# A new order for the first 512 tokens of a sketched attention with a Swish MLP behind it, and keys turned into a layout with contiguous rows

## The chip, the cores and the metric

The kernel runs on one NeuronCore of a Trainium2 chip. Five engines work side by side, each through its own queue in program order: TensorE (PE in the profile, with its weight loads as PEld), VectorE (DVE), ScalarE (ACT), GpSimd (POOL) and SyncE (SP, which here only issues DMAs). The metric is device time in microseconds of one execution.

## What is computed

Attention with a polynomial sketch: each query and key of 32 numbers is multiplied by two 8x32 matrices, and the 64 products of the two results are its feature vector. Keys and values are summed once per batch and head, and every query reads that sum. The result, 4352 tokens of 128 numbers, goes through an MLP of width 2048 with the gate `h * sigmoid(beta * h)`.

```python
def phi(x):
    a = np.einsum('rd,bhsd->bhsr', S1, x)
    b = np.einsum('rd,bhsd->bhsr', S2, x)
    return np.einsum('bhsi,bhsj->bhsij', a, b).reshape(*x.shape[:-1], r * r)
q_p, k_p = (phi(q), phi(k))
kv = np.einsum('bhsf,bhsd->bhfd', k_p, v)
z = np.sum(k_p, axis=2)
num = np.einsum('bhsf,bhfd->bhsd', q_p, kv)
den = np.einsum('bhsf,bhf->bhs', q_p, z)[..., None] + 1e-06
x = (num / den).transpose(0, 2, 1, 3).reshape(B * S, H * D)
h = x @ w_in
out = (h * (1.0 / (1.0 + np.exp(-beta * h)))) @ w_out
```

There are 4 batches, 4 heads and 1088 positions per head, so 4352 tokens.

## The kernel before

The order of all work is written out by hand in one string of short names, `SEQ`, at the top. Each name issues the instructions of one step on its engines; each engine takes its instructions in that order, and semaphores make it wait for what it reads.

**The attention, per batch b.** `lk`, `lq`, `lv` load keys, queries and values (SP). `tk` turns the keys with DVE transposes (`turn_k`, L456), `kp` multiplies them with the sketches on PE (`kps`, L475), `ka` turns the result back on DVE (`kab`, L492). `ov`/`op` form the 64 products per key on DVE or POOL (`outer`, L513; batch 0 in nine pieces, the others in four), and `v` sums them with the values on PE (L537). Queries: `tq` on DVE (L462), `qp` on PE (L597), `qa` on DVE (L609), denominators `dp` and `di`, a scaling `as`, products `yv`/`yp`, a turn `t` (L640), and `n` on PE (`num`, L653), from which `x` copies tokens into `xT` in fp16 (L665). For batches 2 and 3 the sum z is a DVE reduction `z` (L524) with `zm` on PE and `wz` on DVE; batches 0 and 1 take it from a Gram matrix (`gr` L715, `gc`, `gd`, `wm`, `wc`).

**The first 512 tokens** take a shorter way of their own, named with A: `aA` and `bA` spread the queries on PE (L685), `cA` copies on ACT, `mA` multiplies on DVE, `dA` is the denominator on PE (`den`, L776), `iA` its inverse on DVE, `nA` the numerator on PE (`num0`, L817), `xA` the product of the two on DVE, straight into `xT` (L828).

**The MLP** runs over nine chunks of tokens, eight of 512 and one of 256. A chunk has eight waves: `W` makes two first products of 128x512 on PE into PSUM (`first`, L432; two buffers of that kind), `G` takes the Silu on ACT (L448; 14 buffers for its results), `V` multiplies by the second matrix (`second`, L399). `E` turns the finished chunk on DVE (L413) and stores it. The weights are scaled by beta first: `up`/`uv` (L341, POOL or DVE, after `be` and `bc` spread beta), `wa`/`wp` (L350, L357).

**Warmers.** `h` issues two matmuls on constants into a part of the PSUM tile `kvz0` that nobody reads (`keep_warm`, L191). The same tile holds batch 0's key-value sum.

Two details matter for the change. In `kps` the moving operand is read with an inner step of 288 elements (`kT2` is [token, sketch position] and four tokens far apart are taken together), and in the first pieces of batch 0 ACT copies half of the key sketch into `kvz0` (`acopy0`, L500), from where DVE's `outer` reads it.

In the order before, `SEQ` has batch 1's keys (`tk1`, `kp1`, `ka1`, `gr1`) and batch 0's other queries mixed into the way to the first `W`, and a `V` follows after five `W`s.

Of the kernel before, what the change touches and what calls it, by code (L numbers as in the profile page):

```python
# [9 lines left out]
F32 = mybir.dt.float32  # L10
# [6 lines left out]
P = 128  # L17

SEQ = """
    lk0 lqA lk1 lv0 h sp h h h h sk s1 bsp s0 h sw h tk0a h h h tk0b li0 tqA kp0b li1 kp0a ka0b lq0  # L20
    aA ka0a ca0b li2 op07 h rb ca0a be0 ov06 lo3 cA0 op05 ov08 h lo0 bA bc0 tk1 op04 lo2 gr0 bc1 h
    op02 lk2 h gc0 h be1 ov01 lo1 up0 ov03 h lq1 sr bc2 ov00 v06 up2 v08 lv1 ztv v03 bc3 v01 mA0 v07
    up1 v00 src cA1 kp1 tq0 zm gdp0 up3 v05 v04 ka1 zc wm0 v02 up5 wc0 h mA1 kd0 gr1 qp0 uv7 gc1
    kda0 dA gdv1 op12 qa00 lv2 h qa01 nd0 h h iA nc0 h up6 h wa10 wa11 h nA dpp0 wa2 wa3 h h op11 h
    xA wa0 wa1 np0 h h h tk2 nca0 W wa6 wa7 op13 h W G h di0 h kp2 tq1 G wm1 op10 lk3 W h lq2 V wa14
    wa15 lv3 W asv0 ka2 up4 wc1 G v11 v10 yv00 v13 G v12 W yv01 kda1 lq3 qp1 t00 op20 G V qa11 wa4
    wa5 op23 np1 W qa10 nca1 W G V t01 dpp1 v23 tq2 G n0 op21 wa12 wa13 di1 op22 W xa01 xv00 V G wp4
    W z20 v21 asp1 G W V yp12 G W z21 V G yp11 W V G W yp13 V t11 G W E0 zm2 v22 G yp10 W wz2 V t13
    G W t10 V G qp2 t12 v20 qa20 V V qa21 n1 tk3 dpp2 V di2 xa10 V xa11 W kdv2 V asv2 G W yp20 V G W
    E1 yp23 kp3 G t20 W ka3 V G W yp22 t23 V G W yp21 np2 V G W V ov32 G W t22 V G ncv2 W ov31 V G  # L30
    t21 op30 W V tq3 G V op33 W E2 n2 G z31 v31 xa21 W V G W z30 V G W V G W v33 xv20 G W v30 zm3 G
    W wz3 V G qp3 v32 qa31 W kda3 V qa30 G W V dpp3 G W V di3 G V W asp3 E3 np3 W G yv30 V yv31 V G
    W yp33 t30 V G W V G W yv32 V ncv3 G W t31 V t32 G W t33 V G W V G n3 E4 W xa31 xv30 V G W V G V
    W V G W V G W V G W V G W V G W E5 V G W V G W V G W V G W V G W V G W V G W V G W E6 V G W V G
    W V G W V G W V G W V G W V G W V G W E7 V G V V V E8
# [4 lines left out]
def kernel(  # L40
# [12 lines left out]
    nc = tc.nc  # L53
# [62 lines left out]
    s16 = sb([2 * R, H, D], F32, "s16")  # L116
    for n, (s_, eng) in enumerate(((S1, nc.sync), (S2, nc.scalar))):
        eng.dma_start(
            out=s16[n * R : n * R + R],
            in_=bass.AP(tensor=s_.tensor, offset=s_.offset, ap=[[D, R], [0, H], [1, D]]),  # L120
        )

    k_t, q_t, v_t = {}, {}, {}

    def load_rows(src, dst, b, tag, parts=((0, T),), eng=None):
        if b not in dst:
            dst[b] = ld.tile([P, T, D], F32, tag=tag, name=tag)
        for t0, t1 in parts:
            (eng or nc.sync).dma_start(
                out=dst[b][:, t0:t1, :],  # L130
                in_=bass.AP(
                    tensor=src.tensor,
                    offset=src[b, 0].offset + t0 * D,
                    ap=[[T * D, P], [1, (t1 - t0) * D]],
                ),
            )

# [50 lines left out]

    def keep_warm(n, fresh=False):
        for _ in range(2 * n):  # L190
            nc.tensor.matmul(  # L191
                out=kvz0[:, TCH - 160 :],
                lhsT=idle,
                rhs=cut(idle, [[0, 5], [1, 32]]),
                start=fresh,
                stop=True,
                skip_group_check=True,
            )
# [22 lines left out]
    nc.gpsimd.memset(kT2[0][:, T:, :], 0.0)  # L221
# [21 lines left out]
    nc.gpsimd.memset(kT2[1][:, T:, :], 0.0)  # L243
# [211 lines left out]
    def turn_k(b, t0=0, t1=T):  # L455
        nc.vector.transpose(  # L456
            out=kT2[b % 2][:, t0:t1].rearrange("p t s -> p (t s)"),
            in_=k_t[b][:, t0:t1].rearrange("p t d -> p (t d)"),
        )
# [8 lines left out]
    def kps(b, j0=0, j1=NJK):  # L468
# [3 lines left out]
        for g in range(4):  # L472
            for pi in range(2):
# [24 lines left out]
    def acopy0(j0, j1):  # L498
        c = F + H * R * j0
        nc.scalar.copy(  # L500
            out=cut(kvz0, [[H * R, j1 - j0], [R, H], [1, R]], c), in_=KAB[0][:, j0:j1, :, :R]
        )

    def outer(dst, b, src, w, nm, nj, j0, j1, eng):
# [6 lines left out]
        if dst is KP and b == 0 and eng is nc.vector:  # L511
            left = cut(kvz0, [[R, n], [1, R], [0, R]], F + H * R * j0)
# [18 lines left out]
    def kv(b, j0, j1):  # L531
# [3 lines left out]
        for j in range(j0, j1):  # L535
            for h in range(H):
# [4 lines left out]
                    start=(summed[b] == 0),  # L541
# [169 lines left out]
    def gram(b):  # L711
        t = PS["gram", b] = one("gram")
        for j in range(NJK):
# [5 lines left out]
                start=(j < 2),  # L719
# [23 lines left out]
    def zmm():  # L743
        t = PS["zc"] = one("zc")
        for h in range(H):
            for c in range(2):
# [4 lines left out]
                    start=True,  # L751
                    stop=True,
                )
# [18 lines left out]
    def den(n):  # L772
        t = PS["den", n] = one("dps")
        w = 16 * QSPR[n][1]
        for h in range(H):
# [4 lines left out]
                start=True,  # L780
                stop=True,
            )
# [81 lines left out]
    DO["tk0a"] = lambda: turn_k(0, 0, 2 * NJK)  # L864
    DO["tk0b"] = lambda: turn_k(0, 2 * NJK, T)
    DO["lk0"] = lambda: load_rows(k, k_t, 0, "k", ((0, 2 * NJK), (2 * NJK, T)))
# [96 lines left out]
```

## Time and profile before

| | |
|---|---|
| Median of 3 runs | 107.05 us (106.26 to 107.45) |
| The profiled execution | 106.79 us, of which the profile's span is 105.0 us |
| DVE, ACT, POOL busy | 60%, 76%, 39% of the span |
| Granted TensorE clock | full throughout |
| HBM read, written | 8.94 MB, 2.23 MB |

The profile is of one execution. A row of the chain of waits gives start, duration, engine, tile and line. A row of the groups gives line, engine, operation, output and input shapes with the count, then the busy time in all, the mean in ns, and the idle time before them. A row of the table by stretches gives the stretch and its length, then busy time and instruction count for PE, PEld, DVE, ACT and POOL, the granted clock, the DMA share and GB/s.

### The profile page before, as it was taken

The page shows a single profiled execution, that of the slowest core. Times are in us where ns is not written, and L with a number is a line of the kernel's source. Part 1 is how long each engine was busy: PE and PEld are TensorE (multiplying, and loading weights), DVE is VectorE, ACT ScalarE, POOL GpSimd, SP SyncE. Part 2 cuts the span into 40 slices and gives each one's busy share as a digit, 9 for nine tenths or more (in the row PEclk, how much of TensorE's full clock was granted, in tenths as well). Part 3 has the DMA queues.
Part 4 walks back from the last instruction along what each step waited for, and adds up shares of the span by engine and source line. Part 5 has one row for each costly group of instructions (what it writes and reads, how often), then busy time and mean ns, then how long its engine had stood idle before and what let it go on. Part 6 is the DMA issues. An engine that isn't in the chain of part 4 may idle for free.

```text
span 105.0 us, 3104 instructions
## 1 busy us (share of the span) xinstructions
PE 98.2 (93%) x1291; PEld 52.6 (50%) x1291; DVE 62.8 (60%) x104; ACT 79.8 (76%) x114; POOL 40.7 (39%) x61
## 2 busy tenths in 40 slices
PE   5996899999999999999999999999999999999950
PEld 5873647463545444542545444454444444445730
DVE  3347586989969999966995953699840020110210
ACT  1506352669899999178999798999969999999920
POOL 7527864893189992229980000381000000000000
PEclk9999999999999999999999999999999999999999
DMA  1999999889460004200500240024014124014054
GB/s 23 316 340 313 365 396 403 268 228 369 149 225 31 21 0 65 41 0 15 85 6 0 35 71 0 0 31 69 0 19 71 16 40 63 6 24 73 2 89 61
DMA packets 23577, 11.37 MB, mean 108 GB/s; under 512 B 19323, under 2 KB 21387, under 8 KB 23563
## 3 DMA queue, kind: packets, MB, share of 16 engines
q1 hardware_dynamic: 22419, 11.08, 38.0%
q10 hardware_dynamic: 1144, 0.09, 0.8%
q8 instruction: 10, 0.16, 0.7%
q14 instruction: 4, 0.03, 0.1%
HBM read 8.94 MB, written 2.23 MB: 106 GB/s over the span
## 4 chain that ended last, share of the span: by engine, by line
PE 88%; DVE 7%; issue 1%; ACT 1%; ACTq 0%
PE wave L432 29%; PE moeout L399 27%; PE kvz L191 9%; PE kvz L537 5%; PE nps L653 4%; PE kps L475 4%; PE qps L597 3%; DVE kp L513 2%; DVE qab L609 1%; PE gram L715 1%; PE nps L817 1%; DVE qT L462 1%; PE ndps L578 1%; DVE qt L640 1%; PE dps L776 1%
## 5 line engine op out<-in xcount | busy, mean ns | idle before, releaser
L448 ACT ACTIVATE g<-wave 128x1024 f16<-128x1024 f32 x68 | 64.2, 1043 | 2.4 <-PE wave L432 1.7
L432 PE MATMUL wave<-xT,winp 128*128 128x512 f16 (+1 forms) x144 | 40.5, 368 | 0.1
L399 PE MATMUL moeout<-g,woutp 128*128 128x512 f16 (+1 forms) x144 | 39.1, 367 | 0.1
L432 PEld LDWEIGHTS <-winp 128*128 128x128 f16 x144 | 15.3, 114 | 15.7 <-issue 5.6
L399 PEld LDWEIGHTS <-woutp 128*128 128x128 f16 x144 | 13.8, 97 | 14.0 <-issue 1.1
L413 DVE STREAM_TRANSPOSE o_sb<-moeout 128x512 f32<-128x512 f32 (+1 forms) x9 | 6.1, 682 | 23.4 <-PE moeout L399 23.4
L513 POOL TENSOR_TENSOR kp<-kab 128x512 f32<-128x512 f32 (+2 forms) x14 | 15.4, 1123 | 7.6 <-PE kvz L537 3.7
L191 PE MATMUL kvz<-idle 128*128 128x160 f16 x82 | 10.2, 278 | 2.5 <-DVE kp L513 1.1
L513 POOL TENSOR_TENSOR qo<-qab 128x512 f32<-128x512 f32 (+1 forms) x9 | 11.2, 1273 | 2.0 <-DVE qab L635 1.9
L191 PEld LDWEIGHTS <-idle 128*128 128x128 f16 x82 | 8.0, 118 | 4.8 <-issue 2.0
L640 DVE STREAM_TRANSPOSE qt<-qo 128x512 f32<-128x512 f32 (+1 forms) x14 | 10.3, 759 | 0.0
L617 POOL TENSOR_TENSOR dpr<-qab 128x288 f32<-128x288 f32 (+1 forms) x4 | 2.9, 728 | 16.6 <-DVE qab L609 16.2
L524 DVE TENSOR_REDUCE zs<-kp 128x128 f32<-128x1152 f32 x4 | 8.5, 2156 | 0.0
L609 DVE STREAM_TRANSPOSE qab<-qps 128x576 f32<-128x576 f32 (+1 forms) x8 | 5.3, 695 | 2.5 <-PE qps L597 2.5
L537 PE MATMUL kvz<-kp,v 128*32 128x64 f32 x288 | 6.5, 222 | 0.2 <-DVE kp L513 0.2
L537 PEld LDWEIGHTS kvz<-kp,v 128*32 128x32 f32 x288 | 4.7, 109 | 3.8 <-issue 3.0
L665 ACT CAST xT<-nps 128x576 f16<-128x576 f32 (+1 forms) x5 | 3.0, 595 | 4.2 <-PE nps L653 4.2
L653 PE MATMUL nps<-qt,nd 32*32 32x288 f32 (+1 forms) x256 | 6.0, 385 | 0.0
L341 POOL TENSOR_TENSOR winp<-w_in_sb,beta_bc 128x256 f16<-128x256 f32 x7 | 5.0, 728 | 1.5 <-DMA w_in_sb<-in_moe_w_in_dram 1.4
L456 DVE STREAM_TRANSPOSE kT<-k 128x1088 f32<-128x1088 f32 (+2 forms) x5 | 5.3, 1069 | 0.0
L462 DVE STREAM_TRANSPOSE qT<-q 128x1088 f32<-128x1088 f32 (+2 forms) x5 | 5.3, 1052 | 0.0
L513 DVE TENSOR_TENSOR qo<-qab 128x512 f32<-128x512 f32 (+1 forms) x5 | 4.8, 986 | 0.0
(103 smaller groups left out, 73.6 us busy)
## 6 DMA issues: line engine op xcount, KB each, us to landing
v<-in_v_dram SPq DMA_DIRECT2D x15, 144.0 KB, 5.2
k<-in_k_dram SPq DMA_DIRECT2D x3, 544.0 KB, 5.3
q<-in_q_dram SPq DMA_DIRECT2D x3, 544.0 KB, 6.8
out_dram<-o_sb SPq DMA_DIRECT2D x20, 64.0 KB, 2.0
w_out_sb<-in_moe_w_out_dram SPq DMA_DIRECT2D x4, 256.0 KB, 7.5
w_in_sb<-in_moe_w_in_dram SPq DMA_DIRECT2D x2, 256.0 KB
w_in_sb<-in_moe_w_in_dram SPq DMA_DIRECT2D x1, 512.0 KB, 7.1
k<-in_k_dram SPq DMA_DIRECT2D x1, 288.0 KB
```

What stands on the lines that cost most here:

```text
L191: nc.tensor.matmul(out=kvz0[:, TCH - 160 :], lhsT=idle, rhs=cut(idle, [[0, 5], [1, 32]]), start=fresh, stop=True, skip_group_check=True,)
L399: nc.tensor.matmul(out=moe["acc"][:, :tw], lhsT=woutp[:, j, :], rhs=g[jj], start=(j == 0), stop=(j == NJ - 1),)
L413: nc.vector.transpose(out=o_sb[:, :nt, :].rearrange("p t d -> p (t d)"), in_=PS["acc", ci][:, :tw])
L432: nc.tensor.matmul(out=wv[:, jj // per, o : o + tw], lhsT=cut(winp, [[step, P]], c), rhs=xT[:, t0 : t0 + tw], start=True, stop=True,)
L448: nc.scalar.activation(out=g, in_=wv, func=ACTF.Silu)
L462: nc.vector.transpose(out=qT2[b % 2][:, t0:t1].rearrange("p t s -> p (t s)"), in_=q_t[b][:, t0:t1].rearrange("p t d -> p (t d)"),)
L513: eng.tensor_tensor(out=cut(dst[b][:, j0:j1], [[F, n], [R, R], [1, R]]), in0=left, in1=cut(a0, [[w, n], [0, R], [1, R]], o + R), op=MUL,)
L524: nc.vector.tensor_reduce(out=RB["zs", b][:, hs].rearrange("p h f -> p (h f)"), in_=KP[b][:, :, hs].rearrange("p j h f -> p (h f) j"), axi ...
L537: nc.tensor.matmul(out=KVZ[b][32 * h : 32 * h + 32, :F], lhsT=v_t[b][:, h, j, :], rhs=KP[b][:, j, h, :], start=(summed[b] == 0), stop=(sum ...
L609: nc.vector.transpose(out=cut(QAB[b], [[32, 2], [32 * H, nq], [1, 32]], 64 * i), in_=cut(PS["qps", b][i], [[512, 2], [1, 32 * nq]]),)
L640: nc.vector.transpose(out=QT[b][:, j0:j1].rearrange("p j h c s -> p (j h c s)"), in_=QO[b][:, j0:j1].rearrange("p j h f -> p (j h f)"),)
L653: nc.tensor.matmul(out=ts[g // 2][32 * h : 32 * h + 32, g % 2, : 32 * nq], lhsT=ND[b][rows, fc, 32 * h : 32 * h + 32], rhs=QT[b][rows, :nq ...
```

## The change

**The order.** `SEQ` is replaced as a whole. What is new in it: all steps of batch 0's keys and of the way A come ahead of batch 1's `kp1`, `ka1`, `gr1` and of batch 0's other queries; only the turn `tk1` stays ahead. The first chunk's eight `W` stand ahead of any `V`; the second chunk's first two do as well, so that up to ten `G` results are held (six before). The loads have a new order. Later on `W` and `V` come in pairs as often as singly. There are 45 `h` in place of 33. Some steps change engine: batch 1's and 2's key products go to DVE in part, batch 0's query products `y` and the scalings `as` to POOL.

**Batch 0's keys** are issued ahead of the sketches, one part from SP and one from ACT.

**The turned keys.** `kT2` becomes [4, 9, 8, 4], so that the 32 columns that one matmul step reads lie side by side; the DVE transpose now writes with an inner step of 4 elements (16 bytes), and takes two instructions per batch where it took one.

**PSUM.** The Gram matrix, `zc` and the denominators of the first 512 tokens move from their own tiles into free columns of `kvz0` (with no start flag, after the first warmers have cleared it); the copied key sketch moves out of `kvz0` into a tile of its own. The warmers write 144 columns in place of 160.

```diff
 SEQ = """
-    lk0 lqA lk1 lv0 h sp h h h h sk s1 bsp s0 h sw h tk0a h h h tk0b li0 tqA kp0b li1 kp0a ka0b lq0
-    aA ka0a ca0b li2 op07 h rb ca0a be0 ov06 lo3 cA0 op05 ov08 h lo0 bA bc0 tk1 op04 lo2 gr0 bc1 h
-    op02 lk2 h gc0 h be1 ov01 lo1 up0 ov03 h lq1 sr bc2 ov00 v06 up2 v08 lv1 ztv v03 bc3 v01 mA0 v07
-    up1 v00 src cA1 kp1 tq0 zm gdp0 up3 v05 v04 ka1 zc wm0 v02 up5 wc0 h mA1 kd0 gr1 qp0 uv7 gc1
-    kda0 dA gdv1 op12 qa00 lv2 h qa01 nd0 h h iA nc0 h up6 h wa10 wa11 h nA dpp0 wa2 wa3 h h op11 h
-    xA wa0 wa1 np0 h h h tk2 nca0 W wa6 wa7 op13 h W G h di0 h kp2 tq1 G wm1 op10 lk3 W h lq2 V wa14
...
+    lq0 h h tk0a bsp h sp sw h h h h lqA tk0b sk s1 s0 kp0b kp0a tq0 ka0b sr src ka0a rb tqA h h h h
+    ca0a ca0b be0 bc1 gr0 aA bA gc0 ov00 ov08 op07 op02 op01 bc0 cA0 ztv gdv0 ov06 lv0 cA1 v01 v08
+    mA0 be1 mA1 h op03 op05 v06 v07 zm v02 wm0 v03 v05 v00 lk1 tk1 op04 li0 bc3 bc2 wc0 zc li2 lo1
+    qp0 qa00 v04 dA up1 up0 kd0 li1 h nd0 h h nc0 up5 up4 iA lk2 lo0 lq1 h h nA h lv1 lk3 lo2 lo3
+    lq3 xA h h up3 qa01 wa4 wa5 kda0 h h h W W G lq2 h up2 uv7 kp1 G lv2 W dpv0 di0 ka1 tk2 h h h h
+    W gr1 up6 G G W h h h h W h gc1 asp0 G yp00 kp2 ov11 ov10 G gdp1 wm1 W wc1 G W h np0 op12 G yp01
+    nca0 tq1 ka2 wa2 wa3 G op13 qp1 t00 t01 v11 v12 v10 h qa10 qa11 wp4 h v13 n0 h ov23 kda1 wa10
+    wa11 h xa01 xa00 h h wa0 wa1 lv3 ov22 dpv1 h op21 np1 h h W W h h op20 di1 tq2 G G V nca1 wa6
...
 """
...
+    load_rows(k, k_t, 0, "k", ((0, 2 * NJK),), nc.sync)
+    load_rows(k, k_t, 0, "k", ((2 * NJK, T),), nc.scalar)
...
-                out=kvz0[:, TCH - 160 :],
+                out=kvz0[:, HC:],
                 lhsT=idle,
-                rhs=cut(idle, [[0, 5], [1, 32]]),
+                rhs=cut(idle, [[0, 9], [1, 16]]),
...
-        kT2.append(sb([P, TPAD, 32], F32, f"kT{n}"))
+        kT2.append(sb([P, 4, NJK, 8, 4], F32, f"kT{n}"))
...
-    def turn_k(b, t0=0, t1=T):
-        nc.vector.transpose(
-            out=kT2[b % 2][:, t0:t1].rearrange("p t s -> p (t s)"),
-            in_=k_t[b][:, t0:t1].rearrange("p t d -> p (t d)"),
-        )
+    def turn_k(b, g0=0, g1=4):
+
+        for a, n, j1 in ((g0, min(g1, 3) - g0, NJK), (3, g1 - 3, T - 3 * NJK)):
+            if n > 0:
+                nc.vector.transpose(
+                    out=cut(kT2[b % 2], [[1, n], [32, j1], [32 * NJK, 4], [4, 8]], a),
+                    in_=k_t[b][:, NJK * a : NJK * a + n * j1].rearrange("p t d -> p (t d)"),
+                )
...
-                    rhs=bass.AP(
-                        tensor=kT2[b % 2].tensor,
-                        offset=kT2[b % 2][rows].offset + 32 * j0 + 8 * g,
-                        ap=[list(kT2[b % 2][rows].ap[0]), [32, j1 - j0], [1, 8], [32 * NJK, 4]],
-                    ),
+                    rhs=kT2[b % 2][rows, g, j0:j1],
...
     def acopy0(j0, j1):
-        c = F + H * R * j0
+        if "a0" not in PS:
+            PS["a0"] = one("a0")
         nc.scalar.copy(
-            out=cut(kvz0, [[H * R, j1 - j0], [R, H], [1, R]], c), in_=KAB[0][:, j0:j1, :, :R]
+            out=cut(PS["a0"], [[H * R, j1 - j0], [R, H], [1, R]], H * R * j0),
+            in_=KAB[0][:, j0:j1, :, :R],
         )
...
-        t = PS["gram", b] = one("gram")
+        t = PS["gram", b] = kvz0[:, GC : GC + 32] if b == 0 else one("gram")
...
-        t = PS["zc"] = one("zc")
+        t = PS["zc"] = kvz0[:, ZC : ZC + 8]
...
-        t = PS["den", n] = one("dps")
+        t = PS["den", n] = kvz0[:, DC : DC + 256]
...
-    DO["tk0a"] = lambda: turn_k(0, 0, 2 * NJK)
-    DO["tk0b"] = lambda: turn_k(0, 2 * NJK, T)
+    DO["tk0a"] = lambda: turn_k(0, 0, 2)
+    DO["tk0b"] = lambda: turn_k(0, 2, 4)
```

More of the change, by code (lines that the diff above doesn't have):

```diff
@@ L30 @@
[L30 to L34, printed above, removed]
@@ L115 @@
     nc.vector.memset(idle, 1.0)
[L116 to L120, printed above, removed]
-        )
     k_t, q_t, v_t = {}, {}, {}
@@ L511, in outer @@
         if dst is KP and b == 0 and eng is nc.vector:
-            left = cut(kvz0, [[R, n], [1, R], [0, R]], F + H * R * j0)
+            left = cut(PS["a0"], [[R, n], [1, R], [0, R]], H * R * j0)
         eng.tensor_tensor(
@@ L540, in kv @@
                     rhs=KP[b][:, j, h, :],
-                    start=(summed[b] == 0),
+                    start=(b > 0 and summed[b] == 0),
                     stop=(summed[b] == NJK - 1),
@@ L718, in gram @@
                 rhs=KAB[b][:, j, :, :R],
-                start=(j < 2),
+                start=(b > 0 and j < 2),
                 stop=(j >= NJK - 2),
@@ L779, in den @@
                 rhs=QP[n][:, h % 2, h // 2, :w],
-                start=True,
+                start=False,
                 stop=True,
+                skip_group_check=True,
             )
```

30 lines of the change are left out of this document (20 added, 10 removed).

## The prediction, made before the changed kernel was run

> **What bounds the kernel now.** I read the page first, then the chain of waits, then the table by stretches.
>
> ```profile
> PE 98.2 (93%) x1291; PEld 52.6 (50%) x1291; DVE 62.8 (60%) x104; ACT 79.8 (76%) x114; POOL 40.7 (39%) x61
> ...
> PE 88%; DVE 7%; issue 1%; ACT 1%; ACTq 0%
> ```
>
> PE carries the chain. But its share counts warmers as work, so I look at where the real work starts and how densely it follows (chain of waits: start, us, what):
>
> ```profile
> 22.90 0.43 PE wave L432 x2
> ...
> 58.65 0.55 PE wave L432 x2
> 59.21 0.43 PE moeout L399 x2
> ...
> 88.75 0.48 PE wave L432 x2
> 89.23 0.43 PE moeout L399 x2
> ...
> 99.32 1.85 PE moeout L399 x16
> 101.19 0.45 DVE o_sb L413
> ```
>
> The first `W` comes at 22.90, and PE ends at 101.17; the 3.8 us to the span's end are the last store. A `W` and a `V` cost 0.43 each; late, a pair takes 0.91, which is the Silu's pace. A `W` right after a step on small tiles costs 0.55, 0.12 more. The row at 59.21 is the 25th `V` (the first of chunk 3), and I use it as a milestone, because `E2` on DVE must come before it. So there are three stretches: the head up to the first `W`, the middle up to the 25th `V`, and the rest. The table by stretches, for DVE's part of head and middle (to the end of `E2`), and for the rest:
>
> ```profile
> 4.32:22.48 18.16, 16.33 (x342) 10.92 (x341) 13.22 (x28) 7.53 (x26) 12.20 (x19) 1.00 0.96 334
> 22.48:57.09 34.61, 34.50 (x537) 16.59 (x535) 30.07 (x45) 30.07 (x42) 22.24 (x22) 1.00 0.31 85
> 59.21:101.17 41.96, 41.94 (x346) 21.02 (x344) 15.99 (x22) 39.35 (x43) 3.50 (x3) 1.00 0.22 34
> ```
>
> In the head DVE works 13.22 of 18.16 us and idles 4.94: it hands each step to PE or ACT and waits. In the middle DVE idles 4.54 of 34.61. In the rest PE is full and ACT nearly so.
>
> **The head.** DVE's waits there, and the groups of its instructions that move:
>
> ```profile
> DVE kab L492 <- PE kps L475: 2.0, 3, 1.3
> DVE sk L292 <- PE sps L270: 1.7, 1, 1.7
> DVE kp L513 <- PE kvz L191: 1.4, 2, 1.0
> ```
> ```profile
> L456 DVE STREAM_TRANSPOSE kT<-k 128x1088 f32<-128x1088 f32 x2 | 2.6, 1301 | 0.0
> L513 DVE TENSOR_TENSOR kp<-kvz,kab 128x256 f32<-128x256 f32 x5 | 1.9, 420 | 2.0 <-PE kvz L191 1.4 <-ACT kvz L500 0.5
> L609 DVE STREAM_TRANSPOSE qab<-qps 128x320 f32<-128x320 f32 x2 | 0.9, 495 | 0.0
> L492 DVE STREAM_TRANSPOSE kab<-kps 128x576 f32<-128x576 f32 x1 | 0.8, 782 | 0.3 <-PE kps L475 0.3
> L456 DVE STREAM_TRANSPOSE kT<-k 128x576 f32<-128x576 f32 x1 | 0.8, 767 | 0.0
> ...
> L341 DVE TENSOR_TENSOR winp<-w_in_sb,beta_bc 128x256 f16<-128x256 f32 x1 | 0.4, 402 | 0.0
> ```
>
> Behind the first `W` go batch 1's `ka1` (0.78), one `qa` (0.50) and one `uv` (0.40), and two `ov` pieces go to POOL (2 x 0.42): 2.52. One `gd` goes and one comes. Two turns are cut in two; the fixed part of a turn, from 1301 ns for 1088 elements and 767 for 576, is 0.17, so 0.2 each. DVE's list is 13.22 - 2.52 + 0.4 = 11.1 us. It starts with batch 0's keys, in before here:
>
> ```profile
> 3.64 0.54 PE sps L270 x2
> ```
> ```profile
> 4.32 0.77 DVE L456 STREAM_TRANSPOSE kT<-k 128x576 f32<-128x576 f32 x1
> ```
> ```profile
> 1.19 0.84 SPq L129 DMA_DIRECT2D k<-in_k_dram  x2
> ```
>
> The two key loads were issued at 1.19 and some 0.4 later, now both at 0.74; the sketches stand behind them on both queues, so `sp` comes later than 3.64 but beside the turns. I take 4.3 again (from 3.9, the issue's gain, to 5.1, if the halves delay each other by one turn). The Trainium skill, "DMA: Bandwidth & Descriptors", section "Issuing engines are not separate DMA queues", says that two issuers save only issue time; by that rule too the start stays near 4.3.
>
> From 4.3 the list ends at 15.4 without a wait. What waits go: the copied sketch leaves `kvz0`, so DVE no longer waits for warmers there (1.4), `sk` stands behind the turns (1.7), and `tq0` fills the first wait for `kps`. What is late next: the copies on ACT ahead of `ov00` (covered by `rb` and `tqA`), and PE's `nA` ahead of `xA`. I give those waits 1.3: `xA` ends at 16.7, first `W` at 17.0, 5.9 us ahead of 22.90. With all of the old idle time it would be 20.6.
>
> The loads and POOL on the way:
>
> ```profile
> 8.42 2.38 POOL L513 TENSOR_TENSOR kp<-kab 128x256 f32<-128x256 f32 x4 [2.40 <-DVE kab L492]
> ```
> ```profile
> L341 POOL TENSOR_TENSOR winp<-w_in_sb,beta_bc 128x256 f16<-128x256 f32 x7 | 5.0, 728 | 1.5 <-DMA w_in_sb<-in_moe_w_in_dram 1.4
> ```
>
> POOL now has six `op0` pieces (6 x 0.60) from about 7.5, then `up1 up0 up5 up4 up3 up2` (6 x 0.73): 15.5, and 16.9 if it waits for `w_in` for 1.4 as before. `up2` is wanted by the third `W`, after 18. So the first chunk's weights are hidden, with 1 us to spare. `q`, `v` and batch 1's keys are moved ahead of `w_in` on SP; nothing on DVE or PE asks for `w_in` itself. The Gram matrix, `zc` and the denominators keep their instructions, only the PSUM tile changes: nothing.
>
> **The middle, on PE.** Between the first `W` and the 25th `V` PE has, by these rows:
>
> ```profile
> 17.50 0.70 PE gram L715 x18
> ...
> 19.63 0.69 PE kvz L191 x10
> ...
> 24.18 1.11 PE kps L475 x16
> ...
> 27.24 1.14 PE kvz L537 x72
> ...
> 41.66 0.70 PE qps L597 x32
> ...
> 43.71 1.53 PE nps L653 x63
> ```
> ```profile
> 32.08 1.18 PE L653 MATMUL nps<-qt,nd 32*32 32x160 f32 x64
> ```
> ```profile
> L475 PE MATMUL kps<-kT,sk 64*32 64x288 f32 x48 | 3.5, 653 | 0.0
> L597 PE MATMUL qps<-qT,sw 32*32 32x288 f32 x96 | 2.3, 413 | 0.0
> ```
>
> One `kps` matmul takes 653 ns and one `qps` 413 over the same 288 columns; the difference is that `kps` reads with a step of 288 elements. With contiguous rows I give `kps` the 0.70 of `qps` in place of 1.11 (bounds: 0.70 and 1.11). The Trainium skill, "SBUF — State Buffer", section "Door 1: The DMA port swizzle", says that SBUF has lines of 16 bytes and that an access which changes the line each time pays. The 653 agrees. But by the same rule the new turn pays, as it writes every 16 bytes; no run here shows such a write on DVE.
>
> Sum: 30 `W` and 24 `V` at 0.43, 23.2; three `kps` and three `qps` at 0.70, 4.2; one Gram matrix 0.70; 200 rows of key-value products (72 + 72 + 56), 3.2; `n` of batches 0 and 1, 2.7; 44 warmer matmuls at 0.069, 3.0; some twelve changes of tile at 0.12, 1.4; small transposes and sums about 0.9. That is 39.3, so 56.3 from 17.0. I add 1.7 for waits (the third to eighth `W` go at the Silu's pace with no `V` to fill, and the second chunk waits for `xa`): **the 25th `V` at 58.0**, 1.2 us ahead of 59.21, with two `W` and one `nps` more already done.
>
> **The middle, on DVE.** Rows of what is added to its 30.07:
>
> ```profile
> L524 DVE TENSOR_REDUCE zs<-kp 128x128 f32<-128x1152 f32 x4 | 8.5, 2156 | 0.0
> ...
> L513 DVE TENSOR_TENSOR kp<-kab 128x512 f32<-128x512 f32 x2 | 1.3, 658 | 0.0
> L513 DVE TENSOR_TENSOR qo<-qab 128x768 f32<-128x768 f32 x1 | 0.9, 917 | 0.0
> ...
> L513 DVE TENSOR_TENSOR qo<-qab 128x512 f32<-128x512 f32 x1 | 0.7, 679 | 0.0
> ```
>
> Batch 3's `z` pair now stands ahead of `E2` (4.3); three key products of 512 (2.0) and one of 768 come, two `yv` of 768 and 512 go (the 768s cancel, minus 0.7); `ka1`, `qa`, `uv` come from the head (1.7); two turns are cut (0.4). Sum 37.8. From 4.3, DVE's whole list is 11.1 + 37.8 = 48.9: 53.2 without a wait. The forecast leaves it 4.8 us of idle time up to 58.0; before it had 4.94 + 4.54 = 9.5 over the same steps. This is the number to watch.
>
> **The rest.** 38 `W` and 44 `V` (35.3), two `nps` (3.1), and 0.5 of small steps: 38.9. Before, from 59.21, the same sum was 40 `W`, 44 `V`, one `nps`, 56 rows of products, one `qps`, 0.2: 39.4, and it took 41.96, so 2.5 went in tile changes and the Silu's pace; with about half of the tile changes I take 2.0. PE ends at 58.0 + 40.9 = 98.9, against 101.17. The tail is the same, so 2.3 us are gained: 104.5 from the profiled 106.79, 104.75 from the median of 107.05, which is 0.26 above it. I say 104.6.
>
> **The rivals** (against 107.05; below 105.98 and above 108.12 count as a change, 1% being about what a measurement of this kernel can tell).
>
> *DVE keeps its waits* (slower). The new order has as many hand-offs; if DVE still idles 9.5 us between 4.3 and `E2`, the 25th `V` comes at 62.7 and PE ends at 103.6: 109.4. It decides from 7.1 us of idle time on (no gain), and at 8.2 it is 1% slower. For it: DVE's idle time in the head was ended by PE five times, and eight `W` ahead of any `V` leave PE nothing to do when `n0` is late. Against it: the waits named above have lost their causes. 0.23.
>
> *The strided write costs DVE.* The nearest row of a strided DVE access is `zs`, 1152 elements in 2156 ns, 1.87 ns each, where a turn pays 1.02; 0.85 x 1088 is 0.9 per batch, 3.7 over four. With 4 us of idle time the milestone is 60.9: 107.5. Half of it would be 105.8. Against it: the instruction's own row, 1301 ns, whose writes are contiguous, and which I take. 0.15.
>
> *The change does not do what it says:* `kps` stays at 1.11. Three times 0.41 on PE: 106. 0.08.
>
> *No new waits at all:* the milestone at 56.3, 103.0. 0.06.
>
> **The numbers.** The forecast has 0.48; its own range is 103.2 to 106.2, from 1.5 us on either side of the milestone. Faster by over 1%: 0.46 of it, 0.06, and parts of the second and third rival, 0.08: 0.60. Slower: 0.21 of the first and 0.02 of the second: 0.23. Within 1%: 0.17. The range is 102.8 to 108.6, which leaves out the worse half of the first rival and the end of the last.
>
> **What would show it.** The first `W` at 17 (20.6 or later: the head kept its waits). `kps` of 288 columns at 0.70 (1.11: wrong). `kT` of 864 and 224 elements at about 1.5 us together (2.3: the second rival). DVE's idle time from its first turn to `E2` under 5 us. The 25th `V` at 58, and PE's end 41 us behind it. If the first `W` is early and the 25th `V` is not, the fault is in the middle.

## The result: slower, and the profile after

The changed kernel takes 113.81 us (median of 4 runs, 111.72 to 116.72) where the kernel before takes 106.94. The ratio is 1.049 (95% interval 1.037 to 1.062); like every ratio below it compares only the runs in the faster of two states (here 112.60 and 111.72 us), so it is smaller than that of the medians. The profiled execution took 112.60 us, of which the span is 110.8 (before 106.79 and 105.0). 104.6 was forecast, between 102.8 and 108.6.

The page after, engine totals and the shares of the chain:

```profile
PE 100.3 (91%) x1315; PEld 55.6 (50%) x1315; DVE 67.9 (61%) x109; ACT 79.6 (72%) x111; POOL 40.1 (36%) x61
...
PE 63%; DVE 24%; DMA 4%; issue 3%; ACT 1%; ACTq 1%; POOL 1%; DVEq 0%
```

PE's share of the chain fell from 88% to 63%, and DVE's rose from 7% to 24%. Where that begins and ends is in the chain itself (start, us, what; its marks can lie up to 0.2 us behind those of the timeline that is used further down):

```profile
22.12 1.05 PE wave L437 x4
...
24.05 0.78 DVE kab L496
...
38.50 4.15 DVE zs L530 x2
...
64.78 0.86 PE moeout L404 x4
...
105.22 1.78 PE moeout L404 x16
107.03 0.45 DVE o_sb L418
```

The first `W` comes at 22.12, hardly sooner than before (22.90) and not at 17.0. From 24 to 50 us the chain runs over DVE, through batch 1's `ka1` and batch 2's reduction. The 25th `V`, the milestone, comes at 64.78 (59.21 before), and PE ends at 107.0 (101.2).

Three marks on PE divide the time: the first `W`, the ninth (the second chunk's first) and the 25th `V`. The table by stretches between them (busy time and count for PE, PEld, DVE, ACT and POOL, then granted clock, DMA share and GB/s), before:

```profile
22.73:34.30 11.57, 11.46 (x254) 5.89 (x251) 10.31 (x17) 10.81 (x21) 7.40 (x10) 1.00 0.56 193
34.30:59.04 24.74, 24.74 (x330) 11.43 (x330) 21.47 (x28) 20.42 (x23) 14.59 (x13) 1.00 0.16 26
```

and after:

```profile
22.12:34.75 12.63, 12.55 (x287) 7.84 (x286) 12.22 (x18) 10.67 (x19) 9.47 (x10) 1.00 0.56 198
34.75:64.62 29.87, 28.27 (x389) 13.34 (x387) 28.74 (x36) 23.21 (x29) 17.16 (x16) 1.00 0.14 24
64.62:107.03 42.41, 41.26 (x327) 20.55 (x325) 13.39 (x23) 37.80 (x41) 0.79 (x1) 1.00 0.22 34
```

The first stretch is 1.1 us longer than before, the second 5.1, the last about the same. In the second both PE (28.27) and DVE (28.74) are busy for nearly all of 29.87 us. Part of what stands there on PE is work that the kernel before had behind it by then: four `V` and 24 rows of key-value products. Another part it did only behind its 25th `V`: two `W`, a query projection and most of batch 3's sum; in exchange one `n` stands later now.

### The profile page after: what moved, and what is told of

Its sections match the earlier page's. It is cut to its first block, busy times and chain, and to the rows that moved or that the text cites. A ratio compares the mean times of both kernels' runs of the same rounds, so it can differ in the third digit from the quotient of the medians.

```text
span 110.8 us, 3152 instructions
## 1 busy us (share of the span) xinstructions
PE 100.3 (91%) x1315; PEld 55.6 (50%) x1315; DVE 67.9 (61%) x109; ACT 79.6 (72%) x111; POOL 40.1 (36%) x61
## 4 chain that ended last, share of the span: by engine, by line
PE 63%; DVE 24%; DMA 4%; issue 3%; ACT 1%; ACTq 1%; POOL 1%; DVEq 0%
PE wave L437 22%; PE moeout L404 22%; DVE zs L530 4%; DMA beta<-in_moe_beta_dram 4%; PE kvz L543 4%; DVE kp L519 3%; PE nps L659 3%; DVE kT L464 2%; DVE qt L646 2%; PE kps L483 2%; DVE qT L470 2%; PE qps L603 2%; PE kvz L196 2%; DVE qab L615 2%; PE aps L691 2%
## 5 line engine op out<-in xcount | busy, mean ns | idle before, releaser
L453 ACT ACTIVATE g<-wave 128x1024 f16<-128x1024 f32 x68 | 65.0, 1038 | 8.4 <-PE wave L437 7.8
L404 PE MATMUL moeout<-g,woutp 128*128 128x512 f16 (+1 forms) x144 | 38.0, 367 | 0.1
L519 POOL TENSOR_TENSOR kp<-kab 128x256 f32<-128x256 f32 (+2 forms) x12 | 12.4, 1060 | 5.7 <-DVE kab L496 5.2
L196 PE MATMUL kvz<-idle 128*128 128x144 f16 x106 | 11.7, 262 | 2.0 <-DVE idle L115 1.1
L519 POOL TENSOR_TENSOR qo<-qab 128x512 f32<-128x512 f32 (+1 forms) x10 | 12.1, 1238 | 0.2
L196 PEld LDWEIGHTS <-idle 128*128 128x128 f16 x106 | 9.2, 114 | 4.8 <-issue 2.2
L464 DVE STREAM_TRANSPOSE kT<-k 128x224 f32<-128x224 f32 (+3 forms) x9 | 8.6, 1050 | 2.4 <-DMA k<-in_k_dram 2.4
L519 DVE TENSOR_TENSOR kp<-kab 128x512 f32<-128x512 f32 (+1 forms) x6 | 5.8, 1002 | 0.0
L623 POOL TENSOR_TENSOR dpr<-qab 128x288 f32<-128x288 f32 x2 | 1.6, 790 | 9.2 <-DVE qab L615 9.2
```

What stands on the lines that cost most here:

```text
L196: nc.tensor.matmul(out=kvz0[:, HC:], lhsT=idle, rhs=cut(idle, [[0, 9], [1, 16]]), start=fresh, stop=True, skip_group_check=True,)
L404: nc.tensor.matmul(out=moe["acc"][:, :tw], lhsT=woutp[:, j, :], rhs=g[jj], start=(j == 0), stop=(j == NJ - 1),)
L453: nc.scalar.activation(out=g, in_=wv, func=ACTF.Silu)
L464: nc.vector.transpose(out=cut(kT2[b % 2], [[1, n], [32, j1], [32 * NJK, 4], [4, 8]], a), in_=k_t[b][:, NJK * a : NJK * a + n * j1].rearran ...
L519: eng.tensor_tensor(out=cut(dst[b][:, j0:j1], [[F, n], [R, R], [1, R]]), in0=left, in1=cut(a0, [[w, n], [0, R], [1, R]], o + R), op=MUL,)
```

## The experiments

All marks below are from the timeline of each profiled execution, in us. The median is of all runs of a kernel, and the ratio is against the kernel before, run beside it on the same chip.

| | first W | ninth W | 25th V | PE ends | median | ratio (95%) |
|---|---|---|---|---|---|---|
| before | 22.73 | 34.30 | 59.04 | 101.15 | 106.94 | |
| after | 22.12 | 34.75 | 64.62 | 106.99 | 113.81 | 1.049 (1.037 to 1.062) |
| e1_old_turn | 21.47 | 35.02 | 65.11 | 107.47 | 112.81 | 1.052 (1.043 to 1.061) |
| e2_warm | 22.18 | 35.39 | 64.90 | 107.27 | 111.18 | 1.032 (1.024 to 1.040) |
| e3_den_own | 20.55 | 33.18 | 63.08 | 105.44 | 111.70 | 1.046 (1.039 to 1.052) |
| f1_v_early | 21.67 | 34.84 | 67.16 | 109.53 | 113.83 | 1.056 (1.049 to 1.063) |
| f2_head | 19.92 | 32.82 | 62.44 | 104.81 | 110.75 | 1.041 (1.033 to 1.049) |
| f3_both | 22.55 | 35.54 | 65.46 | 107.83 | 112.36 | 1.053 (1.046 to 1.061) |
| g1_z_cut | 19.20 | 32.52 | 60.84 | 103.22 | 109.40 | 1.028 (1.020 to 1.035) |
| f4_hold_v | 22.27 | 33.58 | 60.04 | 102.14 | 108.15 | 1.011 (1.008 to 1.015) |
| g2_keys_late | 20.32 | 35.89 | 60.63 | 102.74 | 108.31 | 1.018 (1.011 to 1.024) |
| h1_both_parts | 20.61 | 36.71 | 63.17 | 105.27 | 109.98 | 1.034 (1.027 to 1.041) |
| e4_before_rows | 22.10 | 33.80 | 58.07 | 100.18 | 106.29 | 0.994 (0.987 to 1.000) |
| g4_rows_again | 22.76 | 34.49 | 58.76 | 100.87 | 106.42 | 0.997 (0.994 to 1.001) |
| g3_rows_psum | 21.08 | 32.83 | 57.10 | 99.21 | 106.31 | 0.993 (0.989 to 0.998) |
| h2_warm | 21.61 | 33.40 | 57.67 | 99.78 | 105.55 | 0.992 (0.988 to 0.996) |

The upper half are variants of the changed kernel, the lower half variants of the kernel before.

### The turned keys back in their old layout

```diff
-        for a, n, j1 in ((g0, min(g1, 3) - g0, NJK), (3, g1 - 3, T - 3 * NJK)):
...
+        nc.vector.transpose(
+            out=kT2[b % 2][:, t0:t1].rearrange("p t s -> p (t s)"),
```

> The changed kernel with the turned keys in their old layout: the DVE transpose writes contiguous rows again in one instruction per batch (two for batch 0), and the key projection reads with a step of 288 elements. All else, the order too, as changed. Theory D (DVE carries the path from the first W to the third chunk's E, and the turn's 16-byte writes cost it 0.85 us per batch): turns of 1.30 us in place of 2.12, E2 on DVE about 3.4 us earlier (60.1 in place of 63.5), and a profiled span of about 107.5 in place of 110.8. The key projection goes back to 1.1 us per half on PE, hidden. Rival O (the new order itself is late, by waits on PE and POOL): E2 moves by less than 1 us and the span stays above 110. Rival P (PE is the bound): the span grows by the 1.5 us that the key projections lose.

Rival O's numbers came. DVE's busy time from its first turn to the end of `E2` fell from 52.7 to 49.9 us, but its idle time there rose from 6.5 to 10.0, and `E2` started at 64.00 in place of 63.49. What DVE saved, it waited out, in part for the key projection; its waits for that, after the change and then here:

```profile
DVE kab L496 <- PE kps L483: 2.1, 3, 1.0
```
```profile
DVE kab L497 <- PE kps L480: 4.0, 4, 2.0
```

So the writes with a step of 16 bytes do cost DVE about what the second rival said, but the layout as a whole does not set the time: what the old one saves on DVE, it loses at the projection on PE. The cost of the turn without the gain of the projection was not run.

### More warmers in the head

```diff
-    lq0 h h tk0a bsp h sp sw h h h h lqA tk0b sk s1 s0 kp0b
+    lq0 h h tk0a bsp h h h h h sp sw h h h h h h h lqA tk0b sk s1 s0 kp0b
```

> The changed kernel with seven more warmer steps: four ahead of the sketch product, three ahead of batch 0's first key projection, where PE stands idle for 0.9 and 0.8 us. Theory C (PE runs its first 15 us at half speed because the idle stretches from 3.9 on keep its clock gate closed; before, it was at full speed from 7.6): matmuls of the Gram matrix 0.05 us apart in place of 0.10, aps and bps in about 1.0 us in place of 2.0, the first W 1.5 to 2 us earlier (about 20.4 in place of 22.1), and the span about 1.5 us shorter (109.3). Rival: the speed is set by something else (the loads, the kind of operand), and matmul spacing and the first W stay; then the span stays at 110.8 or grows by the few tenths by which warmers delay the key projection.

The head of the changed kernel ran at half speed on PE. Its row of clocks on the page shows nines from the start, but the trace has no entry of the clock ahead of 15.33 us, where it says full speed, and the operations until then are slow. In the kernel before that first entry is at 6.36 us, so the "full throughout" of its table holds from there only: 18 warmer matmuls from 4.17 on took 2.42 us, 0.13 each, and ten from 19.63 on 0.069 each. Batch 0's Gram matrix (timeline), before, after, and in this run:

```profile
11.01 0.77 PE L715 MATMUL gram<-kab 128*64 128x32 f32 x18
```
```profile
10.83 1.28 PE L721 MATMUL kvz<-kab 128*64 128x32 f32 x18
```
```profile
9.24 0.77 PE L721 MATMUL kvz<-kab 128*64 128x32 f32 x18
```

With the warmers the first part of the head went as the theory said: DVE's product behind the Gram matrix started at 10.26 in place of 12.36, and the turn of batch 1's keys at 12.97 in place of 15.96. Then PE stood still, for a reason that the profile does not show, and its clock fell to half for 6.8 us in the middle of work (the timeline of PE, and the table by stretches):

```profile
14.82 0.54 PE L543 MATMUL kvz<-kp,v 128*32 128x64 f32 x23 [1.45 <-issue]
```
```profile
5.50:15.70 10.20, 8.16 (x244) 6.23 (x242) 9.03 (x18) 4.94 (x16) 6.54 (x12) 1.00 0.91 277
15.70:22.50 6.80, 5.82 (x74) 3.52 (x57) 3.67 (x9) 1.42 (x5) 3.46 (x5) 0.50 1.04 401
```

The second row has the clock at 0.50. So the first `W` of this execution came no sooner; the two runs at a mean clock of 1.0 took 110.44 and 109.97, about 2 us less than the changed kernel's 112.60 and 111.72. The half speed is real, and worth up to 3 us in the head. The Trainium skill, "TensorE: Matmul & The Clock Gate", Part 1 (the section on the HAM clock gate), says that the clock is given by windows of some 3.4 us, which run free of the kernel's start; the 6.8 us here agree with two of them.

### The denominators in their own tile

```diff
-        t = PS["den", n] = kvz0[:, DC : DC + 256]
+        t = PS["den", n] = one("dps")
```

> The changed kernel with only the denominators of the first 512 tokens back in a PSUM tile of their own, as before the change. Theory T (waits are kept per tile: in the warmers' tile the turn dT on DVE waits for warmers issued ahead of it, and ended 1.06 us late): dT starts at 18.5 in place of 19.6, the first W about 1.0 us earlier (21.1), the span 0.5 to 1 us shorter. Rival: dT or the product with the inverse waits for something else just behind (the numerator on PE, ACT's copies), and the first W moves by less than 0.3 us.

Right as to the wait. After the change, the turn of the denominators on DVE waited; here it follows the instruction before it at once (timeline of DVE in the changed kernel, then here):

```profile
19.57 0.45 DVE L795 STREAM_TRANSPOSE dT<-kvz 128x256 f32<-128x256 f32 x1 [1.06 <-ACT nd L817]
```
```profile
17.80 0.41 DVE L794 STREAM_TRANSPOSE dT<-dps 128x256 f32<-128x256 f32 x1
```

The releaser that is named was not it: here ACT's copy `nd` starts at 18.30, after the turn. The wait had ended 0.1 us behind the last of three warmer steps into the same tile. The first `W` came 1.6 us sooner, of which 0.6 were there at the turn of batch 1's keys already: this execution had PE at full speed from 3.9 to 7.4 us and at half speed from there to 14.2. In the time of the runs the gain is not clear of the noise (ratio 1.046 against 1.049).

### Second products early, and the head mended

The order of the first (shortened), with six `V` in place of the warmers, and of the second:

```diff
-    up3 qa01 wa4 wa5 kda0 h h h W W G lq2 h up2 uv7 kp1 G lv2 W dpv0 di0 ka1 tk2 h h h h
-    W gr1 up6 G G W h h h h W h gc1 asp0 G yp00 kp2 ov11 ov10 G gdp1 wm1 W wc1 W h np0 op12 G yp01
+    up3 qa01 wa0 wa1 kda0 h h h W W G lq2 up2 uv7 wp1 kp1 G lv2 W wp2 dpv0 di0 ka1 tk2 V
+    W gr1 up6 G G W V wp3 W gc1 asp0 G yp00 kp2 V ov11 ov10 G gdp1 wm1 W wc1 W V np0 op12 G yp01
...
```
```diff
-    lq0 h h tk0a bsp h sp sw h h h h lqA tk0b sk s1 s0 kp0b kp0a tq0 ka0b sr src ka0a rb tqA h h h h
+    lqA h h tk0a bsp h h h h h sp sw h h h h h h h lv0 tk0b sk s1 s0 kp0b kp0a tqA ka0b lq0 sr src ka0a rb h h h h
...
+        t = PS["den", n] = one("dps")
```

> The changed kernel with six second products V moved from behind the ninth W into the stretch between the first and the ninth, in place of all warmers there (the scaled weights that they need are made earlier, three pieces of them on POOL, and two loads of w_out change places). The rest of the order stays. Theory V (the first chunk's eight W without any V leave PE only warmers to run, since W goes at the Silu's pace; the V left over are then in the way behind the ninth W, where PE is dense): first W and ninth W stay at 22.1 and 34.8, the 25th V comes 2.6 us earlier (six pairs of 0.43: 62.0 in place of 64.6), the span is about 108.2. Rival D (DVE's list up to E2 sets the pace of the middle): the 25th V moves by less than 1 us. Rival S (the extra V push the W, or the weights' copies push the Silus on ACT): the ninth W comes over 1 us later and eats the gain.

> The changed kernel with the three causes in the head mended that the first runs point to: the denominators in their own tile; warmers that fill PE's idle stretches up to the first key projection; and batch 0's values loaded ahead of its later queries, whose turn goes behind the first key products on DVE. Theory C+T (PE at half speed, then the late values, then the wait of dT on the warmers' tile): no idle time of PE over 1 us between 11 and 15, dT at about 16 in place of 19.6, the first W at about 18.5 in place of 22.1, the span about 3 us shorter (107.5). Rival: W8 does not follow the first W (it hangs on POOL's and DVE's lists for batch 0's other queries, or PE turns to half speed again later), and the span gains less than 1 us.

> The head of the last run and the early V of the one before it together. If both theories hold, the gains add: first W at 18.5, 25th V at about 58.5, span 104.8, which is level with the kernel before (105.0). If the new order is worse for a reason not named yet, the span stays over 107.

The early `V` failed as a cure. The ninth `W` came at 34.84, as before the cure, so the room was there; but behind it PE arrived early at batch 2's sum and waited 1.95 us for DVE's reduction (1.34 after the change), and in the profiled execution its clock fell to half once more (table by stretches):

```profile
44.60:51.40 6.80, 6.80 (x96) 2.42 (x89) 5.30 (x8) 1.94 (x4) 0.79 (x1) 0.50 0.15 24
```

Half of 6.8 us is 3.4, more than the 2.6 of the six pairs; but a run at a mean clock of 0.999 took 113.03, no better than the changed kernel. The mended head brought 2.2 us of the 3.6 hoped for: first `W` at 19.92, and everything behind it about 2 us sooner, up to the end. It is still 4.1% slower than the kernel before, with a first `W` 2.8 us ahead. So the head explains a smaller part.

The two together were no faster than the changed kernel, but that is no clean test of whether the gains add. PE stood still for 2.26 us at 13.9, again for no reason that the profile names, and then ran at half speed up to 22.1 (table by stretches); the first `W` came at 22.55:

```profile
15.32:22.14 6.82, 6.02 (x104) 3.46 (x105) 3.29 (x7) 1.58 (x6) 5.19 (x8) 0.50 1.05 403
```

All four runs of this kernel had a mean clock between 0.966 and 0.982.

### Batch 2's reduction cut short

In the kernel with the mended head, only 3 of the 9 key positions are summed for batches 2 and 3; the kernel leaves out the rest of these two sums.

```diff
-            in_=KP[b][:, :, hs].rearrange("p j h f -> p (h f) j"),
+            in_=KP[b][:, :3, hs].rearrange("p j h f -> p (h f) j"),
```

> The changed kernel with the mended head of the run before, in which DVE's reductions for batches 2 and 3 leave out two thirds of the sum (3 of 9 key positions are summed): each takes about 0.75 us in place of 2.15, with all waits and the order left. Theory Z (with batch 1's keys and more of the products on DVE, DVE's list reaches batch 2's reduction about 4 us later than before the change, and PE's queue stands behind it at 42.7 with everything that follows): PE's wait ahead of the sum's matmuls (1.1 us) goes, and the 25th V comes 1.1 to 3 us earlier than 62.4, the end with it. Rival L (PE's own list is the bound behind the ninth W, and the wait there is only time that PE loses elsewhere): the 25th V moves by less than 0.5 us.

The matmuls that need the sum, on PE, with the mended head and then here:

```profile
40.49 0.32 PE L555 MATMUL kvz<-zs,ones 128*32 128x64 f32 x8 [1.06 <-DVE zs L530]
```
```profile
38.95 0.29 PE L555 MATMUL kvz<-zs,ones 128*32 128x64 f32 x8
```

The wait is gone, and from the ninth `W` to the 25th `V` it takes 28.3 us in place of 29.6. DVE gains 3.2 us by each pair of reductions and PE only 1.3. With the mended head PE was busy for 28.3 and DVE for 28.4 of the 29.6 us, here PE for 28.1 of 28.3 and DVE for 23.0: both were near their limit, and with DVE's load taken away PE's is left.

### The two parts of the order, one at a time, in the kernel before

The first holds four `V` back, the second moves batch 1's keys, and batch 2's turn `tk2` with them, behind the first `W`; the third does both.

```diff
-    ... W h lq2 V wa14 wa15 ... G V qa11 ... W G V t01 ... xa01 xv00 V G wp4 W z20
+    ... W h lq2 h h h wa14 wa15 ... G h h h qa11 ... W G h h h t01 ... xa01 xv00 h h h G wp4 W V V V V z20
```
```diff
-    src cA1 kp1 tq0 zm gdp0 up3 v05 v04 ka1 zc ... kd0 gr1 qp0 uv7 gc1 kda0 dA gdv1 op12 qa00
-    ... h h op11 h xA wa0 wa1 np0 h h h tk2 nca0 W wa6 wa7 op13 h W G h di0
+    src cA1 tq0 zm gdp0 up3 v05 v04 zc ... kd0 qp0 uv7 kda0 dA qa00
+    ... h h h xA wa0 wa1 np0 h h h nca0 W kp1 ka1 tk2 wa6 wa7 gr1 op12 op11 op13 W gc1 gdv1 G h di0
```

> The kernel before with only its first four V held back behind the ninth W, three warmer steps in the place of each. It is the part of the change that puts the first chunk's waves ahead of any second product, alone. Theory V: the ninth W stays at 34.3, four pairs of 0.43 come behind it, the 25th V and the end 1.7 us later (span 106.7). Rival: PE has room behind the ninth W and the span moves by less than 0.5 us.

> The kernel before with only batch 1's keys (their projection, turn back, Gram matrix and key products) moved from ahead of the first W to behind it, as the change does; all else as before. Theory K (what the head gains comes back behind it, since the same steps stand in the way of batch 1's and 2's sums): the first W about 1 us earlier (21.7 in place of 22.7), batch 2's reduction about 2 us later (ending at 40.5 in place of 38.5), the end 0.5 to 2 us later (span 105.5 to 107). Rival (the change's own claim): the earlier first W carries through and the span is about 1 us shorter (104).

> The kernel before with both of its order's parts changed at once: the first four V held behind the ninth W, and batch 1's keys behind the first W. Theory A (the two losses add, as one takes PE's fill and the other delays what the ninth W waits for): ninth W at 35.9, 25th V at 61.6 to 62.3, span 107.6 to 108.3, about 3% over the kernel before. Rival (they share one wait, as warmers or V are beside the same idle time): the span stays at the 106.6 of the late keys alone.

In the old order, most of the loss can be made with these two parts. With the `V` held, the ninth `W` comes no later, and they stand behind it (timeline of PE):

```profile
33.58 0.59 PE L432 MATMUL wave<-xT,winp 128*128 128x512 f16 x2
34.01 1.89 PE L399 MATMUL moeout<-g,woutp 128*128 128x512 f16 x8
```

From the ninth `W` to the 25th `V` it takes 26.46 in place of 24.74: 1.72 more, which is four times 0.43. PE ends 1.0 us later, as the ninth `W` was 0.7 sooner in this execution. With the keys late, the first `W` comes 2.4 us sooner (I had expected 1), and the ninth 1.6 us later:

```profile
20.32 0.59 PE L432 MATMUL wave<-xT,winp 128*128 128x512 f16 x2
23.73 0.62 PE L432 MATMUL wave<-xT,winp 128*128 128x512 f16 x2
...
35.89 0.59 PE L432 MATMUL wave<-xT,winp 128*128 128x512 f16 x2
```

Between the first and the second `W` PE now has the key projection and the wait for the Gram matrix, 3.4 us, and everything behind the ninth `W` follows at the same distance as before (24.74). What the head gains is given back with 1.6 us on top, since the ninth `W` does not hang on the first: it waits for batch 0's other tokens, whose steps stand on PE, DVE and POOL behind the very keys that were moved. Of the 4.0 us that are lost between the first and the ninth `W`, 0.84 are in this execution a standstill of PE at 28.8 for which the profile names no reason. Both parts together cost 3.4% (1.1% and 1.8% alone): within their intervals they add. The ninth `W` is at 36.71, 0.8 later than with the late keys alone, and 26.46 follow up to the 25th `V`.

### The rest of the change, in the kernel before

The layout alone (twice, one edit), then with the copied key sketch in its own tile and the Gram matrix and `zc` in the warmers' tile, then with three more warmer steps as well. Other than the expectation for the tiles says, the copy of the Gram matrix (`gc0`) kept its old place in the order; only the sketch for it (`sr`, `src`) comes earlier.

```diff
-    ... h sw h tk0a h h h tk0b ... ka0b lq0 aA ... lq1 sr bc2 ... v00 src cA1
+    ... h sw h tk0a h h h h h h tk0b ... ka0b lq0 sr src aA ... lq1 bc2 ... v00 cA1
...
-        c = F + H * R * j0
+        if "a0" not in PS:
+            PS["a0"] = one("a0")
```

> The kernel before with only the new layout of the turned keys (strided DVE write, contiguous read on PE); order, loads and PSUM tiles as before. Theory D: DVE pays 0.85 us per batch (3.4 over four); it idled 9.5 us between 4.3 and E2, so part of it is hidden; the key projection saves 0.4 us per half on PE. I expect 1 us more than the kernel before (108), with the loss already in the head, where batch 0's and 1's turns stand ahead of the first W. Rival P (PE carries the chain, so the projection's saving counts and DVE's loss is hidden): about 1.2 us less (105.8).

> The kernel before with the new layout alone, a second time, with more rounds, to settle its ratio: by its first run (0.9936, 0.9869 to 1.0002) between 0.990 and 0.997 of the time before, if the saving on PE counts and DVE's loss is hidden; 1.000 or more if that was chance.

> The kernel before with the new layout of the turned keys and, of the PSUM moves, those that free DVE from the warmers: the copied key sketch in a tile of its own, the Gram matrix and the batch's z in free columns of the warmers' tile (the copy of the Gram matrix ahead of the next warmers); the denominators keep their own tile; the sketch for the Gram path is copied a little earlier. Order otherwise as before. Theory T (a read from the warmers' tile waits for warmers): DVE's 1.4 us of waits for warmers ahead of the key products go, the first W comes 0.5 to 1 us earlier than the 22.1 of the layout alone, the span is about 103.5. Rival: the waits only move to the next hand-off (values, Gram matrix), and the span stays at the 104.0 of the layout alone.

> The kernel before with the new layout and the PSUM moves, and three more warmer steps ahead of the first key projection, where PE stood idle for 0.8 us. Theory C (an idle stretch of PE early in the head can put its clock to half for 3.4 us or more later; the runs of the version without these warmers had a mean granted clock between 0.963 and 1.0, and the lower ones took over 106 us): mean clocks over 0.99, median about 105.3, ratio about 0.987. Rival: the low clocks come from elsewhere (the late idle stretches) and the spread stays, median 106.3.

The layout alone is at best a small gain, where I had expected a loss of 1 us: 0.994 and 0.997, both intervals touch 1. With the tiles it is 0.993 (0.989 to 0.998), and with the warmers 0.992 (0.988 to 0.996), the fastest here; that is a gain under 1%. With the tiles the profiled span was 103.1 (103.5 had been forecast), but this was the fastest of twelve runs; their median is above it, by the clocks below. DVE's waits in the head, between 4 and 24 us, in the kernel before and with layout and tiles:

```profile
DVE kp L513 <- PE kvz L191: 1.4, 2, 1.0
```
```profile
DVE kp L516 <- ACT a L502: 0.3, 1, 0.3
```

The wait for warmers went, and the key products wait only for ACT's copy now. As to the clocks: without the added warmers 6 of 12 runs had a mean granted clock below 0.99, with them 4 of 11. Theory C's clocks over 0.99 did not come in those four, and whether the warmers help at all cannot be told from so few runs. In time the clock counts: the seven runs of the last kernel at 0.993 or more took 104.7 to 106.0 us, the four others 106.6 to 107.9.

## Why the prediction was wrong

**The head, 5.1 of the 8.1 us** by which PE ended later than forecast (107.0 against 98.9). The step that failed is "I give those waits 1.3". DVE's part of the head after the change:

```profile
4.91 2.12 DVE L464 STREAM_TRANSPOSE kT<-k 128x576 f32<-128x576 f32 x3 [2.38 <-DMA k<-in_k_dram]
...
8.51 0.85 DVE L496 STREAM_TRANSPOSE kab<-kps 128x256 f32<-128x256 f32 x2 [0.82 <-PE kps L483]
...
12.36 0.57 DVE L738 TENSOR_TENSOR zt<-gsb,mk 128x256 f32<-128x256 f32 x1 [1.53 <-ACT gsb L732]
...
14.76 0.69 DVE L709 TENSOR_TENSOR qp<-aps,asb 128x512 f32<-128x512 f32 x1 [1.38 <-ACT asb L703]
...
15.96 2.23 DVE L464 STREAM_TRANSPOSE kT<-k 128x864 f32<-128x864 f32 x2
```

The waits, with the one for `dT`, are 0.82, 1.53, 1.38 and 1.06: 4.8 us, 3.5 more than I gave. The two turns took 4.35 us in place of 3.1, and the start was 0.6 later; that makes 5.3 (`xA` ended at 22.07 in place of 16.7). Two of these waits, at `zt` and at the product `mA`, end with ACT's copies of what PE made at half speed. I took PE's durations from a trace in which it was at full speed from 6.4 us on, and did not ask whether the new order keeps it so: it moves the sketches behind the keys, and PE stands idle from 3.9 to 4.8 and from 6.4 to 7.2 with its warmers spent. The fourth was priced at nothing ("only the PSUM tile changes: nothing"), although the row of 1.4 us that I quoted as going away was the same wait, for warmers in a shared tile.

**The turn.** I took the row with contiguous writes. The rows after, groups by shape:

```profile
L464 DVE STREAM_TRANSPOSE kT<-k 128x864 f32<-128x864 f32 x3 | 5.3, 1762 | 0.0
...
L464 DVE STREAM_TRANSPOSE kT<-k 128x224 f32<-128x224 f32 x4 | 2.3, 573 | 0.0
```

1762 and 573 ns are 2.3 us in place of 1.5: the second rival's price, 0.8 to 0.9 per batch. The Trainium skill, "SBUF — State Buffer", "Door 1: The DMA port swizzle", had it: by its rule the new turn pays, and the trace agrees. But its price did not make the time: with the old layout, which takes away the cost and the projection's gain together, the changed kernel was no faster (1.052 against 1.049).

**The projection** was right: 414 ns a matmul in place of 653.

```profile
L483 PE MATMUL kps<-kT,sk 64*32 64x288 f32 x48 | 2.2, 414 | 0.2 <-DVE kT L464 0.2
```

**The middle.** From the first `W` to the 25th `V` I forecast 41.0 us and 42.5 were measured. By the two rows of the table by stretches PE was busy for 40.8 us of it and idle for 1.7. The 1.7 is what I had added for waits, but by luck: 1.34 of it is one wait, for batch 2's reduction, which I had not named. The missing 1.5 are in PE's own list, 40.8 in place of 39.3; which terms were too small was not taken apart. (That at the 25th `V` one `nps` more would be done than before is a slip in the prediction: it is one fewer, two in place of three, and the sums have it right.) DVE's list came to 52.7 us where I had 48.9; the missing 3.8 are mainly the turns (8.6 us in place of the 6.1 that I counted) and the products for batch 0's and 1's denominators, which moved from POOL to DVE (0.32 and 1.32) and which I overlooked. Its idle time was 6.5 us, more than the 4.8 forecast but below the 7.1 from which the first rival would decide. That rival had the direction right, but of the 6.2 us by which `E2` ended late (64.2 in place of 58.0) only 1.7 are idle time; 3.8 are the longer list and 0.6 the start. And `E2` was the wrong mark: DVE is late at batch 2's reduction already, which ended at 42.65 against 38.49.

**The rest** was forecast at 40.9 and took 42.4, as long as before (42.1). The half of the tile changes that I took off did not come back as time. 1.1 of the 1.5 us are two waits of PE of 0.55 for tokens that ACT copies, at 68.6 and 84.1; the kernel before has no such wait behind its 25th `V`.

**What the sum did not ask.** By my own numbers the change carried 3.6 us behind the first `W` (5.9 gained at the first `W`, 2.3 left at the end), and gained only if the head gave back more. The experiments price two parts of that in the old order: the late keys gain 2.4 us at the first `W` and lose 4.0 by the ninth, and the held `V` put 1.7 behind it. I had seen the second ("eight `W` ahead of any `V` leave PE nothing to do when `n0` is late") and left it in a rival as an argument; the sum has waits of 1.7 for it, and no price for the `V` that then stand in a full stretch. Put into the old order, these two cost 3.4%, where the whole change costs 4.9%. In the changed kernel itself the share of the `V` is not shown: six of them put back brought nothing there, and the keys were not put back. For the rest, DVE's longer list (1.3 us at the reduction) and what is left of the head are the likely parts, but that is argued; how it divides, and what the other moves of the order do (key products on DVE, other products on POOL, the loads, the pairs of `W` and `V`), was not measured one by one.

## What to carry to other kernels

The first instruction of a stage is not the mark to optimise where the stage has a second input: ask what its second chunk waits for, and whether the moved work stands ahead of that. When an engine runs fillers in place of real work, price that by the work that must then be done in a stretch with no room. And a change that leaves PE idle twice for 0.8 us early can cost up to 3 us by half speed: read the spacing of equal matmuls, not only the row of clocks.

## What the runs showed of the hardware

In five profiles, all of variants of the changed kernel, PE's clock fell to half in the middle of the work: for 6.8 us in four (7.4 to 14.2, 15.7 to 22.6, 15.3 to 22.1, 44.6 to 51.4) and for 3.4 us in the kernel with the mended head, with PE busy throughout:

```profile
14.82:18.23 3.41, 3.41 (x71) 1.91 (x62) 2.56 (x7) 1.01 (x5) 3.41 (x6) 0.50 1.06 422
```

In the 3.4 us ahead of these falls PE was busy for 1.4 to 2.4 us. But with the early `V` it was busy for only 1.9 us of the 3.4 from 34.3 on, and no fall came behind that, so these profiles give no sharp limit. It is not the new order alone: of the 12 runs of the old order with layout and tiles, 6 had a mean clock below 0.99, of the 58 runs of the kernel before beside all experiments one (0.984, 110.40 us).

In eight profiles PE stood still for 0.5 to 2.3 us in the middle of a chain of matmuls, with no semaphore to wait for (the longest, in the kernel with both cures):

```profile
13.64 0.22 PE L543 MATMUL kvz<-kp,v 128*32 128x64 f32 x1
16.12 0.87 PE L543 MATMUL kvz<-kp,v 128*32 128x64 f32 x23 [2.26 <-issue]
```

Each time the records of the instruction queue have a load of 16 KB that began up to 2 us earlier (here at 13.79, and it took 0.96, while the data queues moved 390 GB/s by the page's row). That PE ran out of instructions there is possible, but only argued: the changed kernel has such a load at 14.42 and no standstill behind it, and no run took the loads away.
